# The last batch's output cut by half blocks of u: groups of four positions by 89 rows

## The chip, the core and the metric

The kernel runs on one core of a Trainium2 chip. A core has five engines with their own instruction streams: TensorE (PE, matrix products; its weight loads are listed apart as PEld), VectorE (DVE), ScalarE (ACT), GpSimd (POOL) and SyncE (SP). SP does no arithmetic here; it issues DMA transfers. Sixteen DMA engines move the data between device memory (DRAM) and the on-chip memory (SBUF, 128 partitions). TensorE writes its results to PSUM, eight banks of 512 float32 in each partition.

The metric is the device time of one execution in microseconds (us), the median over several runs. A profile is one further execution, with its own time.

## The reference

Eight sequences of 5,696 positions and 128 channels pass through a long convolution and then a spectral mixing layer:

```python
batch, seq, d_model = (8, 5696, 128)
# 1. long convolution with h along the sequence
Yf = np.fft.rfft(x, n=2*S, axis=1) * np.fft.rfft(h, n=2*S, axis=0)[None, :, :]
x  = np.fft.irfft(Yf, n=2*S, axis=1)[:, :S, :]
# 2. 64 low frequencies are mixed over the channels
X = np.fft.rfft(x, axis=1)
Xr, Xi = np.real(X[:, :64]), np.imag(X[:, :64])
Y[:, :64] = (Xr @ w_r - Xi @ w_i) + 1j * (Xr @ w_i + Xi @ w_r)   # one matrix per frequency
u = x + np.fft.irfft(Y, n=S, axis=1)
# 3. a channel product, a ReLU and a sum
return (u + np.maximum(u @ w_ch, 0.0)).astype(np.float32)
```

The output is 8 x 5,696 x 128 float32, 23.3 MB.

## The kernel before, in words

The sequence length is split as 5,696 = 89 x 64: position = 64 q + p, with `NQ` = 89 values of q and `J` = 64 of p. The convolution is done as products with small Fourier matrices. Its forward part (the first 260 us) works on pairs of batches, writes spectra in float16 to a DRAM scratch `zscr`, and ends with the frequency mix. What the change touches comes after that.

**The last phase.** The four pairs of batches are taken in turn (`g_` = 0 to 3). For each pair the scratch is read back in four blocks of 16 values of p (`c_` = 0 to 3), each as two transfers: `ZT..a` with 128 rows of 8 KB and `ZT..b` with 52 rows of 8 KB. Five buffers are loaded ahead. `u_tile(i, b, half)` (line 754) makes u for eight values of p and all 89 of q, with the 128 channels in the partitions: two products with 356 columns and sixteen with 89, into the two banks of one PSUM slot. It then copies the slot as float16 to `u_sb`, at positions 64 q + p, on ACT or DVE. This is a half block; a batch has eight.

`o_tile(g_, b, r4)` (line 808) makes one tile of output. It needs channels last, so u is the stationary operand: `j` runs over four products, each with 128 positions as the weight load (a step of `NW` = 44 positions between them) and the 128 x 256 matrix `WI` streaming, which holds the channel weights beside the identity. Each product gives u w_ch and u side by side. ACT takes the ReLU to a buffer `r_sb` (line 837), DVE adds u (line 838) into an output buffer. A batch has 5,696 = 128 x 44 + 64 positions: eleven full tiles (partition q' holds positions 44 q' to 44 q' + 43, four to a tile) and a tail of 64 rows. Because the 128 rows of one tile lie 44 positions apart, every tile reads all of u, and so waits for all eight half blocks of its batch.

**Output buffers and transfers.** Two tiles next to each other share one buffer of `o8_sb` (seven of them, taken in turn) and go out in one transfer of 128 rows x 4 KB. Single ones have buffers of 2 KB rows. For the last batch of all, the tiles 8 to 10 each go out alone from such a wide buffer, 128 rows x 2 KB, and the tail as 64 rows x 512 bytes. SP issues all of these, in the order of the program.

**The order of the work** is written out by hand: a list `todo` holds the tiles that can be made, and after each half block some of them are taken from its front. For the first three pairs the blocks of both batches alternate, and one or two tiles of the pair before follow each half block. The last pair takes all blocks of batch 6 first and then those of batch 7. Two tiles follow each half block during batch 6, two and three alternately during batch 7. Batch 6's twelve tiles join the list when its last block is done, batch 7's twelve when the loop is over.

Each engine works through its own stream in order, and waits on semaphores that a recorder places from what each operation reads and writes. A tile takes one of four PSUM slots in turn, shared between half blocks and output tiles, so TensorE can run about four items ahead of ACT and DVE.

Of the kernel before, what the change touches and what calls it, by code (L numbers as in the profile page):

```python
# [4 lines left out]
P = 128  # L5
# [4 lines left out]
ADD = mybir.AluOpType.add  # L10
# [3 lines left out]
RELU = mybir.ActivationFunctionType.Relu  # L14
# [109 lines left out]
def bass_long_conv_fft__then__afno_spectral_mix_kernel(nc, x, h, moe_w_r, moe_w_i, moe_w_ch, out):  # L124
    B, S, D = x.shape
    M = moe_w_r.shape[0]
    assert D == P and M == 64 and B == 8
    J = 64
    NQ = S // J
# [3 lines left out]
    NP = B // 2  # L133
# [72 lines left out]
    def at(name, cols, dt, off):  # L206
        return nc.alloc_sbuf_tensor_at(name, [P, cols], dt, offset=off)
# [45 lines left out]
    ZB = 16  # L253
# [13 lines left out]
    u_sb = [at(f"UT{i}", S, F16, u_off[i]) for i in range(4)]  # L267
# [3 lines left out]
    NO8, NO = len(o_big), len(o_off)  # L271
    o8_sb = [at(f"O{i}", 1024, F32, o_big[i]) for i in range(NO8)]
    o_sb = [at(f"Os{i}", 512, F32, o_off[i]) for i in range(NO)]
    r_off = [a_g + 16384 + 2048 * i for i in range(3)]
    NR = len(r_off)
    r_sb = [at(f"R{i}", 512, F32, r_off[i]) for i in range(NR)]
# [12 lines left out]
    def pv(bank, off, dims, p0=0, n=P):  # L289
        return bass.AP(ps, p0 * 4096 + bank * 512 + off, [[4096, n]] + [list(d) for d in dims])  # L290

    R = Recorder(nc)
# [3 lines left out]
    def bank(i):  # L296
        return ("bank", i)
# [18 lines left out]
    def dma(eng, dst, src, ring, reads=(), writes=(), after=()):  # L316
        R.add(eng, lambda h_: h_.dma_start(dst, src), reads, writes, ring=ring, after=after)  # L317

    def mm(o, l, r, st, sp, reads, writes):
        R.add("tensor", lambda h_: h_.matmul(o, l, r, start=st, stop=sp), reads, writes)  # L320
# [3 lines left out]
    def once(key, toks):  # L324
        if key in first:
            return []
        first[key] = 1
        return list(toks)
# [3 lines left out]
    def turns(name, items):  # L332
        i = ring2.get(name, 0)
        ring2[name] = i + 1
        return items[i % len(items)]
# [62 lines left out]
    W1, W2, WI = wc_sb[:, 0:P], wc_sb[:, P:2 * P], wi_sb[:, :]  # L398
# [17 lines left out]
    for j in range(16):  # L416
        t = turns("h", [0, 2, 4])
# [85 lines left out]
    def load_zt(i, eng="sync", more=()):  # L503
        g_, c_ = divmod(i, J // ZB)
        for part, (p0, r0, n) in enumerate(((0, 0, P), (PB, P, RB))):
            old = list(once(("zt", i % NC, part), zt_old[i % NC][part])) + list(more) + pace
            dma(eng, bass.AP(zt[i % NC][part], p0 * ZP, [[ZP, n], [1, ZP]]),
                bass.AP(zs, (g_ * 2 * NK + r0) * J * 256 + c_ * ZB * 256, [[J * 256, n], [1, ZP]]),
                "q" if eng == "gpsimd" else "t", [("zd", g_, s_) for s_ in range(NT)], [("zt", i % NC, part)], after=old)
# [212 lines left out]
    LSLOT = [0, 2, 4, 6]  # L722
    NCH = J // ZB
# [30 lines left out]
    def u_tile(i, b, half):  # L754
        g_, c_ = divmod(i, NCH)
        t = ahead.get((i, b, half))
        if t is None:
            t = u_z(i, b, half)
        else:
            for hb in range(2):  # L760
                u_c(i, b, half, t, hb, False)
        ub = (g_ % 2) * 2 + b
        old = {0: WT, 1: WT, 2: U_ALL, 3: U_ALL}[ub]
        n_ev[0] += 1
        e = "scalar" if n_ev[0] % 8 in (0, 2, 3, 5, 7) else "vector"
        src = pv(t, 0, [[1, NQ], [512, 2], [NQ, 4]])
        evac(bass.AP(u_sb[ub], c_ * ZB + half * 8, [[S, P], [J, NQ], [4, 2], [1, 4]]),
             src, [bank(t), bank(t + 1)], [("u_", ub, 2 * c_ + half)], eng=e, after=once(("u", ub), old))
# [16 lines left out]
    for hb in range(2):  # L785
        evac(bass.AP(y_sb, hb * 32 * B, [[2 * M * B, P], [B, 32], [M * B, 2], [1, B]]),
             pv(6 + hb, 0, [[2 * B, 32], [B, 2], [1, B]]), [bank(6 + hb)], [("y", hb)], eng="vector" if hb else "scalar",
             after=ZY)
    for b in range(B):
        bk = 6 + b // 4  # L790
# [10 lines left out]
    n_o = [0]  # L801
    o_cur = [0]
    o8_old = [H_ALL] * 2 + [U_ALL] + [G_ALL + ZX] * 2 + [WT] * 2
    o_old = [H_ALL] * 2 + [M_ALL[5:6], U_ALL + [("f1",)]]
    NW = S // P
    TAIL = S - NW * P

    def o_tile(g_, b, r4):
        ub = (g_ % 2) * 2 + b
        bb = 2 * g_ + b  # L810
        t = turns("l", LSLOT)
        i = n_o[0]
        n_o[0] += 1
        full = r4 < NW // 4
        last_ = (g_, b) == (NP - 1, 1)
        wide = r4 < (8 if last_ else NW // 4 // 2 * 2)
        big = wide or (last_ and full)
        h_ = r4 % 2 if wide else 0
        if big:
            if not h_:  # L820
                o_cur[0] = turns("o8", list(range(NO8)))
            ob, key, old = o8_sb[o_cur[0]], ("o8", o_cur[0]), o8_old[o_cur[0]]
        else:
            k_ = turns("os", list(range(NO)))
            ob, key, old = o_sb[k_], ("os", k_), o_old[k_]
        OW = 1024 if big else 512
        n, rows = (4, P) if full else (1, TAIL)
        rd = [("u_", ub, c_) for c_ in range(2 * NCH)] + [("wch",), ("i16",)]
        for j in range(n):
            lh = bass.AP(u_sb[ub], 4 * r4 + j, [[S, P], [NW, P]]) if full else u_sb[ub][:, NW * P:S]  # L830
            mm(pv(t + j // 2, (j % 2) * 256, [[1, 256]], 0, rows), lh, WI, True, True, rd, [bank(t + j // 2)])
        bk = [bank(t), bank(t + 1)] if full else [bank(t)]
        rs = r_sb[i % NR]
        rv = bass.AP(rs, 0, [[512, rows], [P, n], [1, P]])
        ov = bass.AP(ob, h_ * 512, [[OW, rows], [P, n], [1, P]])
        src_r, src_u = pv(t, 0, [[256, n], [1, P]], 0, rows), pv(t, P, [[256, n], [1, P]], 0, rows)
        R.add("scalar", lambda e: e.activation(rv, src_r, RELU), bk, [("r", i % NR)], after=once(("r", i % NR), G_ALL + XTT + [("y", 0), ("y", 1), ("id",)]))  # L837
        R.add("vector", lambda e: e.tensor_tensor(ov, src_u, rv, ADD), bk + [("r", i % NR)],  # L838
              [key + (h_,)], after=once(key, old))
        if wide and not h_:  # L840
            return
        w_ = (2 if wide else 1) * 4 * D
        if full:
            dst = bass.AP(out.tensor, out.offset + bb * S * D + (4 * r4 - 4 * h_) * D, [[NW * D, P], [1, w_]])
            src = ob[:, 0:w_]
        else:
            dst = bass.AP(out.tensor, out.offset + bb * S * D + NW * P * D, [[D, TAIL], [1, D]])
            src = ob[0:TAIL, 0:P]
        dma("sync", dst, src, "o", [key + (v_,) for v_ in range(h_ + 1)])

    todo = []
    NB = NCH * NP
    NW4 = NW // 4 + 1
    for g_ in range(NP):
        last = g_ == NP - 1
        order = [(c_, b) for b in range(2) for c_ in range(NCH)] if last else [(c_, b) for c_ in range(NCH) for b in range(2)]
        for n, (c_, b) in enumerate(order):
            i = NCH * g_ + c_
            for half in range(2):
                u_tile(i, b, half)  # L860
                for _ in range((2, 2 + half)[n >= NCH] if last else 1 + half):
                    if todo:
                        o_tile(*todo.pop(0))
            if b == 1 and i + NC < NB:
                load_zt(i + NC)
            if last and n == NCH - 1:
                todo += [(g_, 0, r4) for r4 in range(NW4)]
        todo += [(g_, b, r4) for b in range(1 if last else 0, 2) for r4 in range(NW4)]
    while todo:
        o_tile(*todo.pop(0))  # L870
    R.add("sync", lambda e: e.nop(), [], [("o8", i, v_) for i in range(NO8) for v_ in range(2)] + [("os", i, 0) for i in range(NO)])

    R.emit()
# [29 lines left out]
```

## Time and profile before

| what | us |
|---|---|
| median of 3 runs | 380.24 (378.93 to 380.40) |
| profiled execution, whole | 383.51 |
| its span, first to last instruction | 381.7 |
| first half block of the last pair | 334.04 |
| last copy of u ends | 367.39 |
| last product starts | 374.7 |
| last add ends | 376.49 |

Over the span TensorE is busy for 95%, VectorE 80%, ScalarE 82%. Busy shares are averages over stages with different limits, and a busy TensorE is a modelled one, since products are pipelined. Times within the span are counted from its start. A line such as L838 is a line of the kernel; many operations are recorded by helpers and so share one line (L320 for all products). "x12" is a count. In a list of groups the numbers behind the bar are busy time and mean ns of one instruction, then the idle time of the engine ahead of it and what ended that. A DMA issue line has the size of one transfer and the median time from its issue to its landing.

### The profile page before, as it was taken

Reading aid. Unit: us, or ns where it says so; the run is one execution under the profiler, and the core shown is the slowest. Engines: PE = TensorE matmul, PEld = TensorE weight load, DVE = VectorE, ACT = ScalarE, POOL = GpSimd, SP = SyncE. Lnnn points to the kernel's source line nnn. Section 1 sums busy time; section 2 is a strip of 40 time slices with the busy share of each in tenths; the row PEclk is TensorE's granted clock in tenths of the full one; section 3 lists DMA queues with packets and bytes.
Section 4 is the critical chain, followed back from the end, with each engine's and each line's share of the span. In section 5 each row is a group of like instructions: output and inputs, shape, how many; then the busy total and the mean of one; then the engine's idle time right before and its main releaser. Section 6 shows DMA issues by size and latency. Waiting matters only on the chain.

```text
span 381.7 us, 11950 instructions
## 1 busy us (share of the span) xinstructions
PE 363.6 (95%) x5107; PEld 280.4 (73%) x5107; DVE 303.7 (80%) x331; ACT 311.9 (82%) x492; POOL 83.9 (22%) x137
## 2 busy tenths in 40 slices
PE   7998989999989999999999899999999999999992
PEld 4898856667856667766668666668898988888871
DVE  7566998998988998889998888766347766777784
ACT  8357989998989998999998899994466777777783
POOL 8400012320823311822203211339000000000000
PEclk9997999999999999999999999996899999999997
DMA  7998589998999996999996599999999999999867
GB/s 137 201 280 349 140 228 227 276 269 238 107 134 228 234 269 167 143 129 250 235 283 119 137 298 251 300 328 406 407 388 402 402 415 414 404 408 378 342 256 313
DMA packets 84560, 103.92 MB, mean 272 GB/s; under 512 B 22126, under 2 KB 68974, under 8 KB 81538
## 3 DMA queue, kind: packets, MB, share of 16 engines
q1 hardware_dynamic: 59643, 67.73, 51.3%
q0 software_dynamic: 24864, 35.43, 44.3%
q8 instruction: 40, 0.66, 0.7%
q14 instruction: 13, 0.11, 0.1%
HBM read 70.61 MB, written 51.12 MB: 319 GB/s over the span
## 4 chain that ended last, share of the span: by engine, by line
PE 82%; ACT 9%; DVE 6%; issue 1%; DMA 0%; DVEq 0%
PE ps L320 82%; ACT As L310 7%; DVE As L314 2%; DVE U L597 1%; DVE Hs L312 1%; ACT R L837 0%; DMA F<-cF 0%; DVE UT L312 0%; ACT UT L308 0%; ACT XT L310 0%; DVE O L838 0%; PE ps L791 0%; ACT Hs L308 0%; DVE Os L838 0%; ACT Ah L310 0%
## 5 line engine op out<-in xcount | busy, mean ns | idle before, releaser
L320 PE MATMUL ps<-U,Wc 128*128 128x512 f16 (+1 forms) x368 | 95.8, 384 | 0.0
L605 DVE TENSOR_TENSOR U<-Xs,Hs 128x2048 f16<-128x2048 f16 (+1 forms) x68 | 80.7, 1189 | 11.5 <-ACT Xs L308 10.0
L308 ACT CAST Xs<-ps 128x1024 f16<-128x1024 f32 (+1 forms) x72 | 69.5, 971 | 7.8 <-PE ps L320 4.8
L838 DVE TENSOR_TENSOR O<-ps,R 128x512 f32<-128x512 f32 x81 | 52.5, 686 | 19.8 <-ACT R L837 12.5
L308 ACT CAST Zs<-ps 128x512 f16<-128x512 f32 (+1 forms) x126 | 66.0, 604 | 0.0
L837 ACT ACTIVATE R<-ps 128x512 f32<-128x512 f32 x96 | 50.9, 573 | 14.6 <-PE ps L320 14.1
L314 DVE TENSOR_SCALAR As<-ps 128x720 f16<-128x720 f32 (+1 forms) x60 | 50.1, 879 | 9.1 <-PE ps L320 8.0
L310 ACT ACTIVATE As<-ps 128x720 f16<-128x720 f32 (+1 forms) x72 | 51.6, 772 | 6.6 <-PE ps L320 5.7
L320 PE MATMUL ps<-F,Xin 128*128 128x180 f16 x512 | 54.5, 255 | 2.6 <-ACT Ah L310 1.0
L320 PEld LDWEIGHTS ps<-F,Xin 128*128 128x128 f16 x512 | 46.8, 156 | 9.3 <-DVE As L314 2.6
L320 PE MATMUL ps<-WI,UT 128*128 128x256 f16 x360 | 52.5, 281 | 0.5 <-DVE O L838 0.4
L320 PE MATMUL ps<-As,M 64*128 64x128 f16 x1440 | 48.9, 217 | 4.3 <-DVE U L597 3.5
L320 PEld LDWEIGHTS ps<-U,Wc 128*128 128x128 f16 x368 | 28.5, 98 | 28.5 <-ACT Zs L308 6.1
L320 PEld LDWEIGHTS ps<-As,M 64*128 64x128 f16 x1440 | 40.5, 94 | 10.9 <-DVE U L597 4.2
L317 POOL DMA_DIRECT2D Xt<-in_x_dram x48 | 24.8, 520 | 102.9 <-PE ps L320 102.2
L605 DVE TENSOR_TENSOR U<-ps,Hs 128x2048 f16<-128x2048 f32 x20 | 45.7, 2283 | 0.0
L308 ACT CAST UT<-ps 128x712 f16<-128x712 f32 x40 | 30.0, 752 | 18.7 <-PE ps L320 18.7
L320 PEld LDWEIGHTS ps<-WI,UT 128*128 128x128 f16 x360 | 39.5, 152 | 4.4 <-issue 2.2
L320 PE MATMUL ps<-IBs,C 128*128 128x356 f16 x128 | 40.8, 328 | 0.4
L320 PEld LDWEIGHTS ps<-G,Zs 128*128 128x128 f16 x492 | 27.3, 97 | 13.3
L308 ACT CAST Zt<-ps 128x512 f16<-128x512 f32 (+1 forms) x58 | 31.0, 606 | 0.1
L320 PE MATMUL ps<-G,Zs 128*128 128x2 f16 (+2 forms) x492 | 30.5, 192 | 0.0
(88 smaller groups left out, 500.3 us busy)
## 6 DMA issues: line engine op xcount, KB each, us to landing
out_dram<-O SPq DMA_DIRECT2D x39, 512.0 KB, 10.4
zscr<-Zs SPq DMA_DIRECT2D x60, 256.0 KB, 6.3
Xt<-in_x_dram POOLq DMA_DIRECT2D x24, 320.0 KB, 6.9
zscr<-Zt SPq DMA_DIRECT2D x28, 256.0 KB, 6.6
W<-wscr POOLq DMA_DIRECT2D x8, 512.0 KB, 5.3
M<-cM POOLq DMA_DIRECT2D x5, 720.0 KB, 20.3
ZT0a<-zscr SPq DMA_DIRECT2D x3, 1024.0 KB, 13.4
Xr<-in_x_dram POOLq DMA_DIRECT2D x8, 320.0 KB, 13.8
```

The lines of the kernel that those rows point to most:

```text
L308: R.add(e, lambda h_: h_.copy(dst, src), reads, writes, after=after)
L310: R.add(e, lambda h_: h_.activation(dst, src, COPY, scale=scale), reads, writes, after=after)
L312: R.add(e, lambda h_: h_.tensor_copy(dst, src), reads, writes, after=after)
L314: R.add(e, lambda h_: h_.tensor_scalar_mul(dst, src, scale), reads, writes, after=after)
L317: R.add(eng, lambda h_: h_.dma_start(dst, src), reads, writes, ring=ring, after=after)
L320: R.add("tensor", lambda h_: h_.matmul(o, l, r, start=st, stop=sp), reads, writes)
L597: R.add("vector", lambda e, b=b, s_=s_: e.tensor_tensor(bass.AP(u_s[i], b * 512, [[2048, P], [1024, 2], [1, n * D]]), s_, hv, MULT), [tok, ...
L605: R.add("vector", lambda e: e.tensor_tensor(uv, src, hv, MULT), bk + [("h", t, 0), ("h", t, 1, 0), ("h", t, 1, J)], [("u", i)])
L837: R.add("scalar", lambda e: e.activation(rv, src_r, RELU), bk, [("r", i % NR)], after=once(("r", i % NR), G_ALL + XTT + [("y", 0), ("y", 1 ...
L838: R.add("vector", lambda e: e.tensor_tensor(ov, src_u, rv, ADD), bk + [("r", i % NR)], [key + (h_,)], after=once(key, old))
```

## The change

The last batch, number 7, gets a tiling of its own in a new function `o_last(c_, half, i)`. A half block of u is eight values of p with all 89 of q. For each half block two tiles (`i` = 0, 1) are made: four products, each with the 89 positions of one p as the weight load (a step of 64 positions between them), then ReLU and add on 89 partitions. Partition q then holds positions 64 q + p for eight neighbouring p, and the pair goes out as one transfer of 89 rows x 4 KB from a buffer of `o8_sb`. So a tile reads one half block, and joins `todo` when that half block's copy is recorded. That makes 16 tiles and eight transfers where there were 12 tiles and eight transfers.

The number of tiles taken after each half block of the last pair becomes three, and four in the last block. Two tiles are left when the loop is over. Batch 6's tiles are made as before. In `o_tile` the special case for the last batch goes away.

```diff
@@ o_tile
-        last_ = (g_, b) == (NP - 1, 1)
-        wide = r4 < (8 if last_ else NW // 4 // 2 * 2)
-        big = wide or (last_ and full)
+        big = wide = r4 < NW // 4 // 2 * 2
@@ new
+    def o_last(c_, half, i):
+        ub, bb, p0 = 2 * ((NP - 1) % 2) + 1, B - 1, c_ * ZB + half * 8
+        t = turns("l", LSLOT)
+        k_ = n_o[0]
+        n_o[0] += 1
+        if not i:
+            o_cur[0] = turns("o8", list(range(NO8)))
+        ob, key, old = o8_sb[o_cur[0]], ("o8", o_cur[0]), o8_old[o_cur[0]]
+        for j in range(4):
+            mm(pv(t + j // 2, (j % 2) * 256, [[1, 256]], 0, NQ), bass.AP(u_sb[ub], p0 + 4 * i + j, [[S, P], [J, NQ]]), WI, True, True,
+               [("u_", ub, 2 * c_ + half), ("wch",), ("i16",)], [bank(t + j // 2)])
+        bk = [bank(t), bank(t + 1)]
+        rv = bass.AP(r_sb[k_ % NR], 0, [[512, NQ], [P, 4], [1, P]])
+        ov = bass.AP(ob, i * 512, [[1024, NQ], [P, 4], [1, P]])
+        src_r, src_u = pv(t, 0, [[256, 4], [1, P]], 0, NQ), pv(t, P, [[256, 4], [1, P]], 0, NQ)
+        R.add("scalar", lambda e: e.activation(rv, src_r, RELU), bk, [("r", k_ % NR)])
+        R.add("vector", lambda e: e.tensor_tensor(ov, src_u, rv, ADD), bk + [("r", k_ % NR)], [key + (i,)], after=once(key, old))
+        if i:
+            dma("sync", bass.AP(out.tensor, out.offset + bb * S * D + p0 * D, [[J * D, NQ], [1, 8 * D]]), ob[0:NQ, :], "o",
+                [key + (v_,) for v_ in range(2)])
+
+    def o_next():
+        e = todo.pop(0)
+        (o_last if e[0] == "q" else o_tile)(*e[e[0] == "q":])
@@ the loop of the last phase
-                for _ in range((2, 2 + half)[n >= NCH] if last else 1 + half):
+                for _ in range(3 + (n == 2 * NCH - 1) if last else 1 + half):
                     if todo:
-                        o_tile(*todo.pop(0))
+                        o_next()
+                if last and b:
+                    todo += [("q", c_, half, v_) for v_ in range(2)]
...
-        todo += [(g_, b, r4) for b in range(1 if last else 0, 2) for r4 in range(NW4)]
+        if not last:
+            todo += [(g_, b, r4) for b in range(2) for r4 in range(NW4)]
     while todo:
-        o_tile(*todo.pop(0))
+        o_next()
```

## The prediction

> **What bounds the kernel now.** I read the windows by stage first, then the chain that ended last, then the DMA issues with their times to landing, and last the shapes on one line of TensorE. Busy times by stage, on one core; the last two columns are the share of the 16 DMA engines that is busy and the GB/s that they move:
>
> ```profile
> 300.00:310.00 10.00, 9.92 (x143) 8.78 (x142) 7.86 (x13) 6.96 (x13) 0.00 (x0) 0.95 1.02 414
> 343.44:368.84 25.40, 24.80 (x301) 20.92 (x302) 19.38 (x32) 19.09 (x37) 0.00 (x0) 0.95 0.84 337
> 368.84:376.49 7.65, 6.00 (x41) 4.45 (x41) 7.59 (x14) 6.48 (x12) 0.00 (x0) 0.95 0.76 301
> 376.49:381.72 5.23, 0.00 (x0) 0.00 (x0) 0.00 (x0) 0.00 (x0) 0.00 (x0) 0.60 0.73 282
> ```
>
> At 300 us TensorE and the DMA engines are both full: 414 GB/s at share 1.02 is 414/16/1.02 = 25.4 GB/s per engine, the price that matters below. In the last group (334 to 376) TensorE stays full while DMA falls to 0.84. In the third line VectorE is full (7.59 of 7.65 us), with the twelve tiles that wait for all of u. In the last nothing computes; 5.2 us go to output transfers alone. The chain that ended last, its pieces in order of time, shows the same end:
>
> ```profile
> 366.64 0.75 ACT UT L308
> 367.39 0.52 ACT R L837
> ...
> 368.84 2.14 PE ps L320 x16
> 370.98 0.08 issue
> 371.06 3.64 PE ps L320 x24
> 374.71 0.02 issue
> 374.73 0.61 ACT R L837
> ```
>
> The last copy of u ends at 367.39, the last product at 374.7, the last add at 376.49, and the span at 381.72. So 14.3 us lie behind the last copy of u. That is all that an earlier start of the last batch can attack. Now the DMA issues (size of one, median us from issue to landing):
>
> ```profile
> out_dram<-O SPq DMA_DIRECT2D x39, 512.0 KB, 10.4
> ...
> ZT0a<-zscr SPq DMA_DIRECT2D x3, 1024.0 KB, 13.4
> ...
> ZT0b<-zscr SPq DMA_DIRECT2D x3, 416.0 KB
> ...
> ZT0b<-zscr POOLq DMA_DIRECT2D x1, 416.0 KB, 7.7
> ```
>
> The reader is to see that the same 416 KB has a landing time from POOL's queue and none from SP's. A landing is told where 16 arrivals of the semaphore belong to a transfer. The trace has 42 arrivals for the three SP transfers, 14 each: 13 engines and one increment for the three that carry nothing. This tile has 52 rows. Its cost agrees: the 1 MB tile before it landed at 343.72 and it at 344.95, 1.23 us, which is 4 rows of 8 KB at 309 ns (that packet's duration) on each of 13 engines; 52 rows over 16 engines would be 3.25 rows, 1.0 us. So a transfer from SP is cut by rows, and 52 rows use 13 engines. They are always the same 13: the time from first to last arrival of a 512 KB output transfer is 5.55 us at 302.22 and 6.81 us at 304.98, with one 52-row transfer between, and 9.67 us after four more. Three engines are left ahead each time.
>
> **The change, part by part.**
>
> *Moved earlier: the output of batch 7.* Today 12 tiles (11 of 4 x 128 rows and a tail of 64) follow the last u. Afterwards 16 tiles of 4 x 89 rows, two per half block, join the queue as soon as their half block is copied, and the loops take three tiles per half block (four in the last block) in place of two, and two or three. At the end two tiles remain. Product, ReLU and add have the same free sizes, so one tile costs the same as a full one today: ACT 573 ns, DVE 686 ns, TensorE 4 products at 112 ns. The surplus is 4.5 to 5 tiles: 2.6 us ACT, 3.2 us DVE, 2.2 us TensorE, on the path as far as TensorE is full.
>
> *When the first new transfer goes out.* One half block of u takes 0.98 us of TensorE and a tile 0.47 (starts of half blocks are 1.46 us apart with one tile, 1.91 with two). Three tiles give 2.39 us. The last group begins at 334.04, so its batch 6 takes 8 x 2.39 - 0.7 (two tails) = 18.4 us, until about 352.5; I take 353 for small stalls. Output buffers do not stop it: a pair needs 1.59 us to make and 1.24 to drain, and the seventh buffer back is free at nearly the same time as needed. The first four half blocks of batch 7 still make the 12 tiles of batch 6 (9.2 us), then the first two new tiles: 362.2 + 0.98 + 2 x 0.47 + 1.2 (today's lag from the last product of a pair to its issue) = 365.3. An issue reaches the engines 1.2 us later (issue 364.70, landed 367.28, of it 1.24 moving), at 366.5.
>
> *What the new transfers cost.* There are 8, each of 89 rows x 4 KB = 364.5 KB, all issued from SP. All transfers from SP in this trace whose arrivals I counted give each engine that they use the same number of rows: 128 as 16 x 8, 64 as 16 x 4, 52 as 13 x 4. 89 is prime; equal shares exist only as 89 x 1 or 1 x 89. If equal shares are the rule, each transfer goes on one engine, and since the engines of a split are the same each time, all eight on the same one, one after the other. The trace shows no 89-row transfer from SP, so this is bounded from both sides. The lower end is six rows each on 15 engines: 6 x 155 = 0.93 us per transfer, less than today's 1.24 for 512 KB. The upper end is 89 x 155 ns = 13.8 us per transfer, where 155 ns is from back-to-back 512 KB transfers, which landed at 357.72, 358.94, 360.18, 361.41 and 362.66, 1.24 us for 8 rows per engine (4 KB packets last 159 ns in median). I take the upper end: it continues what 128, 64 and 52 show, while the lower needs unequal shares, which no transfer from SP shows.
>
> [...]
>
> *Sum.* 8 x 13.8 = 110.4 us on one engine from 366.5: 476.9, and 0.3 to the end of the span: 477.2. TensorE is done near 375, so the engine's queue sets the end and all compute differences are covered by it. Against the span of 381.72 this is +95.5 us. The profiled execution took 383.51 us (1.79 around the span), 3.3 above the median of the runs shown; the difference is put on the median: 380.24 + 95.5 = 475.7, so 476 us.
>
> *The other edits.* The eighth pair uses the first one's output buffer (seven in turn), so its add waits until the first transfer has landed, 365.3 + 1.2 + 13.8 = 380.3. Behind it on DVE is only its partner, and on SP only the last transfer and the final wait; the engine has six transfers left then, so the wait costs nothing under one engine, and 5 us or so if it drained faster. On SP the new issues stand behind no others than batch 6's, whose transfers are gone by 366; POOL has nothing in this stage. The weight loads of 89 columns at a step of 64 elements are not in the trace. Nearest rows:
>
> ```profile
> L320 PEld LDWEIGHTS ps<-WI,UT 128*128 128x128 f16 x142 | 15.6, 154 | 3.0 <-issue 1.2 <-ACT R L837 1.1
> ...
> L320 PEld LDWEIGHTS ps<-S4b,ZT0b 84*128 84x128 f16 x32 | 2.8, 98 | 0.4
> ...
> L320 PEld LDWEIGHTS ps<-WI,UT 128*64 128x64 f16 x4 | 0.4, 106 | 0.6 <-issue 0.3 <-ACT UT L308 0.2
> ```
>
> 64 columns took 106 ns and 128 packed columns 98, so a count other than 128 is slower per column: 89 columns would be 147 ns, and 228 with the factor 154/98 of a step. Against the 112 ns of a product that is 0 to 116 ns each over 64 products, 0 to 7.4 us; a gain is excluded, as a load under the product already costs nothing. Only the first 8 lie ahead of the first transfer, so the forecast moves by at most 0.9 us; I take 0.3.
>
> [...]
>
> **The rivals.**
>
> *All engines are used (7 in 100).* The transfer is cut into uneven shares, six rows on 15 engines. Then TensorE sets the end: 353 + 8 x 0.98 + 11.3 x 0.47 + 64 x 0.114 to 0.147 = 373.5 to 375.7, the last add 1.3 later, issue to landing 2.1, end 0.4: a span of 377.3 to 379.5, 2.2 to 4.4 us less than today, so 376 to 378 us; with the slowest weight loads 383. For it speaks that 52 rows alone would also be 13 engines if shares were rounded up to four; against it that no SP transfer shows an uneven share. The point from which it decides: the eight transfers must drain in the 11 us between first and last issue, so at least 8 x 364.5 KB / 25.4 GB/s / 11 = 10.4 engines must take part.
>
> *One engine each, but a different one each time (6 in 100).* Then the transfers overlap. The eighth add still waits for the first landing at 380.3, its transfer is issued at about 381.7 and lands 15 us later: span 397, time 395. Against it speaks the growing lead of the three unused engines.
>
> *Another pace of a lone engine (4 in 100).* If one engine alone were at twice the packet time, the sum would be 220 us in place of 110, time 586; if it went faster by half, 437. For it speaks only that the trace never shows an engine alone.
>
> **How the numbers follow.** One engine for all eight: 83 in 100. Its own ends: 150 ns per row (from the 4 and 8 KB packets, 309 - 159) gives 106.8 us and 168 ns (twice the 84 ns of a 2 KB packet) 119.6 us; the first transfer may go 3 us earlier, if the loop is no slower than today's, or later by as much for full output buffers. That is 469 to 488, and 467 to 490 with the weight loads and the spread of the runs; it holds 80 in 100 of all cases. Faster by over 0.5% (what a measurement of this kernel can tell from no change): 4 in 100, from the first rival; within 0.5%: 3, its slower part; slower: 93, all the rest.
>
> **What the profile after would show.** The eight transfers from SP as 356.0 KB issues with no landing time, for want of 16 arrivals, 13.8 us apart at their landings; the DMA share at 0.06 and 26 GB/s over the last 95 us with every engine idle and the last add near 382; TensorE's last product near 375; before 365 little change but three tiles per half block. The prediction is wrong if these transfers have 15 or 16 arrivals, if their landings overlap, or if the spacing is not near 13.8 us.

## The result and the profile after

The changed kernel takes 483.25 us in the median of 5 runs (481.96 to 483.65), the kernel before 379.98 us beside it. The ratio is 1.272 (95% interval 1.269 to 1.275), a loss of 103 us. The forecast was 476 us in a range of 467 to 490. The profiled execution took 481.96 us, with a span of 480.1 us.

Busy times by stage of the changed kernel, with the same columns as before: batch 6 of the last pair, batch 7 up to the first new transfer, the rest of the computing, and the end.

```profile
331.25:352.50 21.25, 19.90 (x235) 16.85 (x235) 16.15 (x26) 15.64 (x31) 0.00 (x0) 1.00 0.98 397
352.50:366.53 14.03, 13.68 (x167) 12.05 (x166) 11.43 (x20) 10.50 (x21) 0.00 (x0) 1.00 0.91 363
366.53:378.00 11.47, 10.34 (x92) 9.91 (x89) 8.42 (x13) 9.07 (x15) 0.00 (x0) 1.00 0.08 27
378.00:480.10 102.10, 0.00 (x0) 0.00 (x0) 1.28 (x2) 0.00 (x0) 0.00 (x0) 0.51 0.06 26
```

In the last line nothing runs for 102 us but two adds, and the DMA engines move 26 GB/s at a share of 0.06. One engine of sixteen is a share of 0.0625. This rate is already there in the third line, while TensorE and VectorE are still at work: from the first new transfer on, all output goes at the pace of one engine. The chain that ended last, its pieces in order of time:

```profile
362.63 2.46 PE ps L320 x26
365.09 0.09 issue
365.19 0.58 DVE O L865
365.77 0.04 issue
365.81 0.70 DVE O L865
366.51 0.02 issue
366.53 16.41 DMA out_dram<-O
382.93 0.03 issue
```

The first pair's add is followed by its transfer, issued at 366.53 and landed 16.4 us later. The chain is read through instructions, so it goes on to the add that waited for that buffer and stops there; the seven transfers still queued at that point stand behind no instruction. In the list of DMA issues and in that of waits they are these lines:

```profile
out_dram<-O SPq DMA_DIRECT2D x8, 356.0 KB
```

```profile
DVE O L865 <- DMA out_dram<-O: 6.0, 1, 6.0
...
DVE O L836 <- DMA out_dram<-O: 2.4, 2, 1.7
```

The issue line has no time to landing, which as before means that fewer than 16 arrivals belong to one transfer. Here each transfer has two, one right behind the end of its issue and one at its landing (for the first one 366.94, with the issue's end at 366.78, and 382.93). The trace's arrival records have the landings at 382.93, 396.77, 410.59, 424.44, 438.25, 452.08, 465.90 and 479.73: 13.83 us apart, each time 89 rows at 155 ns. In the trace's packet records from 371 us on the 4 KB rows start 155 ns apart in median.

### The profile page after: what moved, and what is told of

It is laid out like the page before. It is cut to its first block, busy times and chain, and to the rows that moved or that the text cites. A ratio compares the mean times of both kernels' runs of the same rounds, so it can differ in the third digit from the quotient of the medians.

```text
span 480.1 us, 11995 instructions
## 1 busy us (share of the span) xinstructions
PE 363.8 (76%) x5126; PEld 282.1 (59%) x5126; DVE 306.0 (64%) x335; ACT 313.9 (65%) x496; POOL 84.3 (18%) x137
## 4 chain that ended last, share of the span: by engine, by line
PE 59%; ACT 7%; DMA 7%; DVE 5%; issue 1%; DVEq 0%
PE ps L320 59%; DMA out_dram<-O 7%; ACT As L310 6%; DVE As L314 2%; DVE U L597 1%; DVE Hs L312 1%; ACT UT L308 1%; DVE O L836 1%; ACT R L835 1%; DMA F<-cF 0%; DVE UT L312 0%; DVE O L865 0%; ACT XT L310 0%; DVEq L105 0%; PE ps L791 0%
## 5 line engine op out<-in xcount | busy, mean ns | idle before, releaser
L320 PE MATMUL ps<-U,Wc 128*128 128x512 f16 (+1 forms) x368 | 94.4, 376 | 0.0
L836 DVE TENSOR_TENSOR O<-ps,R 128x512 f32<-128x512 f32 x70 | 45.7, 686 | 18.1 <-ACT R L835 11.1
L320 PE MATMUL ps<-WI,UT 128*128 128x256 f16 (+1 forms) x379 | 56.0, 286 | 1.1 <-DVE O L836 1.1
L320 PE MATMUL ps<-F,Xin 128*128 128x180 f16 x512 | 52.8, 249 | 2.7 <-ACT Ah L310 1.0
L835 ACT ACTIVATE R<-ps 128x512 f32<-128x512 f32 x84 | 44.2, 572 | 14.5 <-PE ps L320 14.4
L320 PEld LDWEIGHTS ps<-F,Xin 128*128 128x128 f16 x512 | 45.1, 155 | 9.6 <-DVE As L314 2.7
L320 PEld LDWEIGHTS ps<-WI,UT 128*128 128x128 f16 (+1 forms) x379 | 44.6, 168 | 3.9 <-issue 2.0
```

## The experiments

**Other cuts of the same rows (e1).** The transfer of a pair becomes two (in the code cuts of this part, angle brackets stand for addresses and "..." for what is left out):

```diff
-            dma("sync", <out, rows of 89>, ob[0:NQ, :], "o", [key + (v_,) for v_ in range(2)])
+            for q0, n_ in ((0, 80), (80, 9)):
+                dma("sync", <out, from row q0, n_ rows>, ob[q0:q0 + n_, :], "o", [key + (v_,) for v_ in range(2)])
```

> The changed kernel with each 89-row transfer cut into one of 80 rows and one of 9, both from SP; all else is the same. Theory (the engines that a transfer gets decide): 80 rows go on 16 engines, 5 rows each, 0.78 us; 9 rows on 9 engines, 0.16 us. The landings follow the issues by 2 to 3 us, the wait of the eighth pair for its buffer (6.0 us) goes, and the span ends about 2.5 us behind the last add: 379 to 384 us, the 98 us are gone. Rival (the tiles of 89 rows or the order of the tiles cost the time, not the transfers): still above 470 us.

Measured: 384.12 us in 6 runs, against 379.86 for the kernel before, ratio 1.011 (1.008 to 1.014). The theory holds: 99 of the 103 us go with the cut alone, with tiles and order untouched. The issues of this kernel from 366 us on:

```profile
out_dram<-O SPq DMA_DIRECT2D x8, 320.0 KB, 2.9
out_dram<-O SPq DMA_DIRECT2D x8, 36.0 KB
```

80 rows land in 2.9 us and have all 16 arrivals; 9 rows have no landing time, so fewer. On how many engines they went was not counted. With both parts in place what is left is a loss of 1.1%, taken up below.

**Sixteen row counts in one run (e2).** Each of the eight transfers is cut at another row, and each part has a semaphore of its own:

```diff
+    CUT = [85, 84, 88, 78, 82, 87, 77, 79]
...
+            for q0, n_ in ((0, CUT[p0 // 8]), (CUT[p0 // 8], NQ - CUT[p0 // 8])):
+                dma("sync", <out, from row q0, n_ rows>, ob[q0:q0 + n_, :], "k", ...)
```

> Each 89-row transfer is cut in two in another way, with a semaphore for each part, so that arrivals tell the engines: 85+4, 84+5, 88+1, 78+11, 82+7, 87+2, 77+12, 79+10 rows. Theory (the largest divisor up to 16): 5, 14, 11, 13, 2, 3, 11 and 1 engines for the first parts, and 4, 5, 11, 7, 2, 12, 10 for the second ones of more than one row; the lowest engine carries 17+6+8+6+41+29+7+79 rows and 8 of the second parts, 201 x 155 ns = 31 us from about 368.5, time about 400 us. Rival (shares rounded up, six rows each): 15, 14, 15, 13, 14, 15, 13 and 14 engines, time 380 to 384. Second rival (any count that is no multiple of 16 goes on few engines, whatever divides it): 84, 78 and 88 rows have no more than one or two.

Measured: 407.32 us. The arrivals, from the trace's records (below 16 engines one arrival more than engines: 14 for the 52 rows, whose 1.23 us is the time of 13 engines, and two for the 89 rows at one engine's pace):

```
rows     85  84  88  78  82  87  77  79 |  4   5   1  11   7   2  12  10
arrivals  6  15  12  14   3   4  12   2 |  5   6   2  12   8   3  13  11
engines   5  14  11  13   2   3  11   1 |  4   5   1  11   7   2  12  10
```

All sixteen are the largest divisor of the row count up to 16. Rounded-up shares would have given 85 rows 15 engines and 82 rows 14; few engines for any count that is no multiple of 16 would not have given 84 rows 14. The pace is seen too: the 79 rows landed 12.2 us after the transfer ahead of them (392.67 to 404.91), 155 ns a row on a single engine. The time is 7 us above the expectation: the engine with the most rows began at about 370.3 and not 368.5, its 31.2 us of rows were spread over 34.8 (the last arrival came at 405.09), and the expectation left out the 2.2 us from that arrival to the end of the execution.

**The same transfers from POOL (e3).** Only the issuing engine differs:

```diff
-            dma("sync", ..., "o", ...)
+            dma("gpsimd", ..., "p", ...)
```

> The changed kernel with the eight 89-row transfers issued from POOL, not SP. Theory A (the cut belongs to the queue: POOL gives rounded-up shares, six rows on 15 engines): each lands 3 to 5 us behind its issue, time 380 to 386. Theory B (89 rows go on one engine from any queue): landings 13.8 us apart, time about 483.

Measured: 388.27 us. Of the two theories only A is near, though the time lies 2 us above its range of 380 to 386. The issues from 366 us on:

```profile
out_dram<-O POOLq DMA_DIRECT2D x8, 356.0 KB, 3.7
```

The 89 rows now land in 3.7 us. Each transfer has 16 arrivals, but from POOL so had the 52-row transfers of the kernel before, so arrivals don't tell the engines here. The packets of the first transfer run from 368.04 to 369.82 us, which is 205 GB/s, about eight times the 26.4 GB/s of one engine. By this estimate about eight engines or more took part; that it was 15 with six rows each is not shown. The divisor, which the sixteen counts of e2 show for transfers from SP, would be one engine for 89 rows; from POOL it doesn't hold.

The span ended at 386.45, 3.7 us after the last landing at 382.77. In the trace's records POOL executes a DRAIN behind its last issue, from 378.71 to 386.22, and all engines stop right after it. Without these 3.7 us the time would lie within the expected range; whether the DRAIN itself waits for something of the transfers is not shown.

**The kernel before with a prime row count (e4).** Its own 128-row tiles and order; the seven full transfers of the last batch are cut at row 127:

```diff
+        if last_ and full:
+            for q0, n_ in ((0, 127), (127, 1)):
+                dma("sync", <out, from row q0, n_ rows>, ob[q0:q0 + n_, 0:w_], "o", ...)
+            return
```

> The kernel before, with its own tiles and order; only the seven full transfers of the last batch are cut into 127 rows and 1. Theory (a prime row count alone makes it): 127 rows on one engine are 127 x 155 ns = 19.7 us for 4 KB rows and 127 x 84 ns = 10.7 us for 2 KB rows, 4 x 19.7 + 3 x 10.7 = 110.7 us and some 1 us for the single rows, from about 368 (today's first issue of the batch at 366.8 to 368.7): span about 482, time about 480. Rival (the tiling or the order of the change is needed for the loss): 380 to 383.

Measured: 485.82 us, span 484.0. So the loss needs nothing of the new tiling; a row count of 127 in seven transfers makes it alone. The time is 6 us above the expectation, mostly because the first 127 rows landed at 392.74 and so began near 373, not 368. The 4 KB ones landed at 392.74, 412.61, 432.51 and 452.40, 19.9 us apart (19.7 and a single row), the 2 KB ones 10.2 us apart.

**What is left of the loss: order, loads, surplus (e5, e6, e7, e9).** All four start from the kernel with 80 and 9 rows.

```diff
# e5: other counts of tiles
-                for _ in range(3 + (n == 2 * NCH - 1) if last else 1 + half):
+                for _ in range((4 if b else 2 + (n == NCH - 1)) if last else 1 + half):
# e6: u of the last batch stored position by position, 89 side by side
+        if g_ == NP - 1 and b:
+            dst = bass.AP(u_sb[ub], (c_ * ZB + half * 8) * NQ, [[S, P], [4 * NQ, 2], [1, 4 * NQ]])
+            src = pv(t, 0, [[512, 2], [1, 4 * NQ]])
...
-            mm(..., bass.AP(u_sb[ub], p0 + 4 * i + j, [[S, P], [J, NQ]]), ...)
+            mm(..., bass.AP(u_sb[ub], (p0 + 4 * i + j) * NQ, [[S, P], [1, NQ]]), ...)
# e7: e5 and e6 together
# e9: e6 without the second tile of the first four half blocks
-                    todo += [("q", c_, half, v_) for v_ in range(2)]
+                    todo += [("q", c_, half, v_) for v_ in range(1 if c_ < 2 else 2)]
...
-        if i:
+        if i or c_ < 2:
```

> The kernel with 80 and 9 rows, and other counts of tiles: two after each half block of batch 6 (three in its last block) and four during batch 7. Theory (with 80 and 9 rows, what is left of the loss is partly the wait of VectorE for output buffers while the DMA engines are full, 2.9 us in two waits during batch 6): these waits go, 1.5 to 3 us less than with three tiles each, 381 to 383 us. Rival (the surplus of work alone sets the end, and the waits are covered): no change, 384.

> The kernel with 80 and 9 rows; u of the last batch is stored with the 89 positions of one p side by side, so that the new weight loads read packed columns. All else is the same. Theory (the loads of 89 columns at 246 ns hold up their products, which start 157 ns apart where those of 128 columns start 112 to 114 apart): loads near 147 ns, products 115 to 147 apart, so 64 x 10 to 42 ns = 0.6 to 2.7 us less, 381.5 to 383.5 us. Rival (VectorE sets the pace of these tiles, at 0.64 us each, so slow loads cost nothing): 384.

> Both of the two kernels beside it in one. Theory: the two gains add up, 379 to 381.5 us, no different from the kernel before or up to 1 us slower. Against a clear gain over the kernel before speaks the sum: 19 products more are 2.2 us of TensorE, and the end behind the last product can shrink from 7.0 us to no less than 4.5. Rival (either the waits or the loads were covered by the other): the better one of the two alone.

> The kernel with 80 and 9 rows and packed loads; the second tile of the first four half blocks of the last batch is left out, so that the last batch has 12 tiles, as before, and half of the rows of those four half blocks isn't computed (the transfers carry what the buffer holds). Theory (the surplus of four tiles is what is left of the loss): 4 x 0.65 = 2.6 us less than with 16 tiles, 380.5 to 381.5 us. Rival (the end behind the last product, or the slots of PSUM, set what is left): 383 to 384.

| kernel | median us | ratio to before (95%) |
|---|---|---|
| e1: 80 and 9 rows | 384.12 | 1.011 (1.008 to 1.014) |
| e5: pace | 383.77 | 1.0105 (1.008 to 1.013) |
| e6: packed loads | 383.6 | 1.009 (1.0065 to 1.012) |
| e7: both | 383.54 | 1.011 (1.008 to 1.0145) |
| e9: e6 with 12 tiles | 381.06 | 1.003 (1.001 to 1.006) |

In e9 half of the rows of four half blocks are not computed; it serves only to price four tiles. The theories on pace and loads fall, though both edits did what they say, and so does the sum of both gains: e7 is no better than either alone. In e1 VectorE waits 2.9 us for output buffers (first fence below); in e5 0.5 us is left, in one wait. The loads fell from 246 ns (e1, second fence) to 121 ns (e6, third).

```profile
DVE O L836 <- DMA out_dram<-O: 2.9, 2, 1.7
```

```profile
L320 PEld LDWEIGHTS ps<-WI,UT 128*89 128x89 f16 x64 | 10.2, 246 | 0.0
```

```profile
L320 PEld LDWEIGHTS ps<-WI,UT 128*89 128x89 f16 x64 | 6.5, 121 | 1.4 <-ACT R L867 0.9 <-issue 0.4
```

Neither moved the end by more than the interval. In e7 the chain shows what came in their place; five lines of it, and the same pattern in most half blocks of the last batch:

```profile
367.24 0.70 DVE O L868
367.94 0.14 issue
368.07 2.47 PE ps L320 x30
370.54 0.04 issue
370.58 0.70 DVE O L868
```

TensorE makes a half block and three tiles in 2.47 us and then waits 0.7 us for an add. Five items per half block go through four PSUM slots, so an add has to free a slot first; whether the slots or VectorE's own work set this pace was not tested. The surplus is the cause that held: with 12 tiles in place of 16 the time is 2.5 us lower than e6 (383.6 to 381.06), near four times 0.65 us of adds. Four times the 0.47 us of TensorE would be 1.9 us, and the intervals are too wide to tell the two apart. Of e6's 0.9% about two thirds is thus the larger number of tiles; the rest, 0.3% (0.1 to 0.6%), stays open. No version tried beats the kernel before.

**The kernel before, once more (e8).** No edit.

> The kernel before, unchanged, profiled once more. Theory (the profiled execution that the prediction was made from had a granted clock of 0.95 over most of its span, which delayed the last group): a granted clock of 1.00 outside short stretches, the last group begins near 331 and not at 334.0, and the span is 377 to 379 us, with about 47 us from that begin to the end. Rival (the clock matters little): begin near 334 and span near 381.7.

Measured: 379.4 us, span 377.6, the last group begins at 331.45. From its windows, the last group until its products are done, and the end:

```profile
331.45:372.96 41.51, 40.25 (x468) 33.49 (x468) 33.01 (x54) 32.20 (x61) 0.00 (x0) 1.00 0.89 359
372.96:377.60 4.64, 0.00 (x0) 0.00 (x0) 1.16 (x3) 0.15 (x1) 0.00 (x0) 0.74 0.79 306
```

The granted clock is 1.00, where the execution that the prediction was read from had 0.95. So the first execution had the lower clock, its last group began 2.6 us later and its span was 4.1 us longer, as the theory has it; the stretch from that begin to the end is 46.2 us here, a little under the 47 expected. Two executions show that these go together, not that the clock is the cause.

## Why the prediction was right

*The step that decides, the engines of an 89-row transfer,* was right, and so was the reason: equal shares, continued from 128, 64 and 52 rows, leave one engine for 89. e2 shows the divisor for sixteen more counts, e1 and e4 that the count alone makes and undoes the loss. Reading the missing landing time of the 52-row line as 13 engines, from 14 arrivals, agrees with e2, where 79 rows had two arrivals and the pace of one engine. The price of 155 ns per row was measured as 13.83 us a transfer against 13.8.

*The first new transfer* was put at 365.3 with the last group beginning at 334.04, that is 31.3 us after it. It was 35.3 us (366.53 from 331.25), and its landing came 16.4 us later, not 15.0. The terms that were too small: batch 6 took 21.25 us, for which I had 18.4 and 0.5 of stalls; "output buffers do not stop it" was wrong by two waits on VectorE (2.4 us in the list of waits), with the DMA engines busy at a share of 0.98. The first four half blocks of batch 7 took 10.1 us, not 9.2. The time from that point to the issue was 3.9 us, not 3.1. And the engine still had earlier output until 368.4, which I took to be gone by 366. Together these are 5.4 us of the 7 us by which the forecast was low; the base, next, gives the rest. So the path was right, and the stages up to the first landing were each taken too short.

*The base.* The sum was made against an execution 3.3 us above its median, with the lower clock (e8), and the result of the change was on the other side, its profiled execution 1.3 us below its own median. If the lower clock delayed the last group but not the transfers, as the two executions suggest, a difference put on the median was not the same for both kernels. In the spans, 477.2 forecast against 480.1, the earlier begin and the slower stage cancel in part.

*The weight loads* of 89 columns at a step of 64 took 246 ns, above the upper end of 228; packed they took 121 ns, below the 147 that was scaled from 64 columns. Scaling by columns from a 64-column load was too steep, and the factor of a step too small (246 to 121 is 2.0, against 154 to 98). Per column that is 2.76 ns at a step and 1.36 packed for 89 columns, 1.66 at a step for 64, 1.20 and 0.77 for 128: 64 and 89 were slower than 128, and other counts are not compared here. As forecast this did not matter for the end.

*The wait of the eighth pair* came (6.0 us, until 382.93 where 380.3 was forecast) and cost nothing, as its transfer was issued at 438.9 and found the engine busy until 465.9.

*The first rival* had the wrong time. With all engines used (e1) the kernel is 1.1% slower, where 376 to 378 us would have been 0.6 to 1.1% faster. In e1's trace batch 6 took 21.8 us (330.77 to 352.53) where 19.0 were taken, the last product began 24.1 us after that where 20.5 to 22.7 were taken, and the last 80 rows landed 3.3 us after their issue, since the transfers ahead were still moving, where 2.1 were taken. A begin 3.3 us earlier than in the execution that the prediction was read from hides part of this. So the 4 in 100 for a gain rested on stages that were taken too short.

*Slips in the working* that change none of this: from the issue at 364.70 to the landing at 367.28, less 1.24 us of moving, is 1.34 us and not 1.2; 147 ns times 154/98 is 231 ns and not 228; the 0.3 us taken for the weight loads is not in the sum; and a lone engine faster by half would have given 439 us, not 437.

## What to carry to other kernels

Before changing a tile's row count, look at the row count of its transfers: from SP 79, 89 and 127 rows, which have no divisor up to 16 but 1, each went on one DMA engine, at 155 ns per row of 4 KB or about 26 GB/s, and the 89-row transfers of one run followed each other on the same engine, 13.83 us apart. In the profile, the issue lines without a landing time (52 and 89 rows from SP) had 14 and two arrivals per transfer, and a stretch with a DMA share of 0.06 was that of a single engine. Cutting the 89 rows into 80, a multiple of 16, and a rest of 9 took 99 of the 103 us away. Also weigh an earlier start against the surplus work that smaller tiles bring: here 103 us came from the row count, and the early start that remained did not pay for four more tiles.

## What the runs showed that I had not expected

SP itself was held while one engine's queue was long. With the eight new transfers (all issues of SP from 360 us on, their start and the time from the first to the last):

```profile
366.53 85.86 SPq L317 DMA_DIRECT2D out_dram<-O  x8
```

The first two issues took 0.25 us each; the third began at 370.05 and took 13.5, and so did most of the later ones, about the time of one transfer on the engine. The third issue ended at 383.55, just behind the first landing at 382.93. In e4 issues of a single row took up to 19.5 us, about the time of one 127-row transfer. Here nothing else was left to issue; whether a load behind such a transfer in SP's stream would wait too, no run here tried.

A transfer of one row of 4 KB (e2) was not spread over its 1,024 elements: its two arrivals, as many as the 79 and 89 rows had, mean one engine.
